# Second MLP of a fused attention kernel: five column passes instead of six, x split in place, operands in one part of SBUF, shorter rings

## The chip, the core and the metric

The kernel runs on one core of a Trainium2 chip. The metric is device time in microseconds (us) of one execution, the median of several runs. TensorE multiplies, VectorE, ScalarE and GpSimd work element by element, SP issues most of the transfers.

## What is computed

Attention over packed queries, then two MLPs on the same 4608 tokens of width 512 (hidden width 2048). The change touches the second MLP alone:

```python
def _moe2_ref(x, w_in, w_out) -> np.ndarray:
    h = x @ w_in
    relu6 = np.clip(h + 3.0, 0.0, 6.0)
    g = h * relu6 / 6.0
    return (g @ w_out).astype(np.float32)

    x = _moe_ref(x=x, **moe_kwargs)
    return _moe2_ref(x=x, **moe2_kwargs)
```

## The kernel before

The first MLP runs in nine blocks of 512 tokens (`block`, with `hidden` at L822 and `project` at L853). It leaves its result x transposed in DRAM, in nine tensors `x1d0` to `x1d8` of 512 columns. Beside it, `Prep` makes the second MLP's weights ready in DRAM.

The second MLP (`class Second`) multiplies with seven products instead of eight on 2 x 2 blocks, in both of its matmuls. A *pass* covers two groups ("halves") of N columns, N = 384, so six passes cover 4608. The two halves are the two block columns; the two halves of the contraction are the two block rows. `x_steps` loads x for a pass (`xr`), forms the differences that the products need, and splits each of the seven operands into a high part (ScalarE, rounded to fp32r) and a low part (VectorE, value minus high part). Both go into one tile, `xc1` to `xc7`. A product of two split operands takes three matmuls: high x high, high x low, low x high.

In a pass, `hidden` (L1031) runs 56 products of 6 matmuls (8 row groups f, 7 products k), applies the activation and leaves `g`. `project` (L1154) is a generator of 28 *steps*, s = 0 to 27, each of 12 matmuls: seven products k in the order 1, 5, 6, 3, 7, 2, 4, and four steps fd for each. So each product is a block of four steps, and at the last of them (s = 3, 7, 11, 15, 19, 23, 27) `after(k)` moves PSUM results out: copies by ScalarE for k = 1, 5 and 2, adds by VectorE for k = 6, 3, 7 and 4, and for k = 7 one add on GpSimd (L1179). An operand of step s is split into a tile `ro` by `split_hi` (ScalarE, L1142) and `split_lo` (VectorE, L1147). Where a product needs a sum of two g blocks, `sums` forms it first.

No scheduler orders this stage: each engine works through its instructions in the order in which the code emits them. In step s of `project` that order is the 12 matmuls, the next weight load, `after(k)` where a block ends, `sums(s + 4)`, the split of step s + 3, one step of `x_steps` for the next pass, and perhaps a `store`:

```python
                self.load_w()
                if s % FD == FD - 1:
                    after(k)
                self.sums(s + 4)
                if s + 3 >= FD:
                    self.split(s + 3)
```

Buffers decide how far ahead this can run: `ro` has four. Weights come through a ring of six tiles `ws` (WS = 6); a tile holds two products of `hidden` or one step of `project`, 12 matmuls either way, and comes in two transfers of 256 KB, one for the first six matmuls and one for the others. After those matmuls `load_w` refills the tile. All these transfers, x and the output stores go through SP's queue in order. x for the next pass is loaded in the middle of `hidden`.

Pools opened with side="right" lie at the upper end of SBUF, the others at the lower end. In the second MLP `ws`, `xr`, `xe` and `xc` are on the right, `ro`, `g` and the rest on the left. In the first MLP `wi`, `wr`, `wo`, `xh`, `xl`, `gh` and `gl` are on the left, `a2h`, `a2l` and `fused` on the right. `hidden` of the first MLP multiplies weight tiles by `a2h` and `a2l`; the weights (products with w_in) lie in `fused` or, for some blocks, in the buffers of `xh` and `xl`.

Of the kernel before, what the change touches and what calls it, by code (L numbers as in the profile page):

```python
# [18 lines left out]
def tile_pack_attention_two_mlps(ctx: ExitStack, tc, q, k, v, p, w_in1, w_out1, w_in2, w_out2, out):  # L19
# [909 lines left out]
    N = 384  # L929
    NPAIR = NBLK * T // (2 * N)  # L930
# [3 lines left out]
    WS = 6  # L934

    class Second:
        def __init__(self):
            right = opened(ctx, "second_r", side="right", reuse_waits="tile")
            self.right = right
            self.prep = None  # L940
            self.extra = []
            self.chunks = self.all_chunks()
            self.loaded, self.used = 0, 0
            self.ws = {}
            self.x = {}
            self.begin = self.x_steps(0)
            self.out = []
# [30 lines left out]
        def x_steps(self, n):  # L978

            xr = self.right.tile([P, KC, 2 * N], F32, tag="xr", name="xr")  # L980
            at_, end = 2 * N * n, 2 * N * (n + 1)
            o = 0
            while at_ < end:
                j, c0 = divmod(at_, T)
                m = min(end - at_, T - c0)
                nc.sync.dma_start(out=xr[:, :, o:o + m], in_=x1d[j][:, :, c0:c0 + m].rearrange("c p t -> p c t"))
                at_, o = at_ + m, o + m
            yield
            b = {(i, k): xr[:, 2 * i:2 * i + 2, k * N:(k + 1) * N] for i in range(2) for k in range(2)}
            e = self.right.tile([P, 2, N], F32, tag="xe", name="xe")  # L990

            def split(k, v):
                t = self.right.tile([P, 2, 2, N], F32R, tag=f"xc{k}", name=f"xc{k}")
                nc.scalar.copy(out=t[:, 0], in_=v)
                nc.vector.tensor_sub(out=t[:, 1], in0=v, in1=f32(t[:, 0]))
                self.x[k] = t


            nc.vector.tensor_sub(out=e, in0=b[1, 1], in1=b[0, 1])
            yield  # L1000
            nc.vector.tensor_sub(out=b[0, 1], in0=b[0, 1], in1=b[0, 0])
            yield
            split(1, b[0, 0])
            yield
            nc.vector.tensor_sub(out=b[0, 0], in0=b[1, 1], in1=b[0, 1])
            yield
            split(6, b[0, 0])
            yield
            split(5, b[0, 1])
            yield  # L1010
            split(7, e)
            yield
            split(3, b[1, 1])
            yield
            nc.vector.tensor_sub(out=b[1, 1], in0=b[1, 0], in1=b[0, 0])
            yield
            split(2, b[1, 0])
            yield
            split(4, b[1, 1])
            yield  # L1020
# [10 lines left out]
        def hidden(self, n):  # L1031
            X, Y, Z, h1, hu, hv = {}, {}, {}, {}, {}, {}
            later = []
# [53 lines left out]
            xs = self.x  # L1087
            for i, (f, k) in enumerate(seq):
# [23 lines left out]
                if i == len(seq) // 2 and self.prep:  # L1112
                    next(self.prep)
# [26 lines left out]
        def split_hi(self, s):  # L1140
            t = self.left.tile([P, 2, 2, N], F32R, tag="ro", name="ro", bufs=4)
            nc.scalar.copy(out=t[:, 0], in_=self.operand(s))  # L1142
            self.ro[s] = t
# [10 lines left out]
        def project(self, n):  # L1154
            X, Y, Z = [], [], []
            o1, ou, ov, o5, oc = (self.left.tile([P, 2, N], F32, tag=tag, name=tag) for tag in ("o1", "ou", "ov", "o5", "oc"))
            last_pair = n == NPAIR - 1
            early = [lambda t=t: self.store(2 * N * n + N + t * P, {0: ou, 1: ov}, t) for t in range(3)]
            if last_pair:
                early += [lambda t=t: self.store(2 * N * n + t * P, {0: oc}, t) for t in range(3)]  # L1160

            def after(k):
                for i in range(2):
                    if k == 1:
                        nc.scalar.copy(out=o1[:, i], in_=X[i])
                    elif k == 5:
                        nc.scalar.copy(out=o5[:, i], in_=Z[i])
                    elif k == 6:
                        nc.vector.tensor_add(out=ou[:, i], in0=o1[:, i], in1=Y[i])
                    elif k == 3:  # L1170
                        nc.vector.tensor_add(out=ou[:, i], in0=ou[:, i], in1=Z[i])
                    elif k == 7:
                        nc.vector.tensor_add(out=ov[:, i], in0=o1[:, i], in1=Y[i])
                    elif k == 2:
                        nc.scalar.copy(out=oc[:, i], in_=X[i])
                    elif k == 4:
                        nc.vector.tensor_add(out=o1[:, i], in0=o1[:, i], in1=Y[i])
                if k == 7:
                    nc.gpsimd.tensor_add(out=ov, in0=ov, in1=o5)  # L1179

            for s in range(FD * S7):
# [26 lines left out]
            for t in range(3):  # L1208
                if last_pair:
                    self.out.append(lambda t=t: self.store(2 * N * n + t * P, {1: o1}, t))  # L1210
                else:
                    self.out.append(lambda t=t: self.store(2 * N * n + t * P, {0: oc, 1: o1}, t))
# [19 lines left out]
        def run(self):  # L1232
            self.left = opened(ctx, "second_l", reuse_waits="tile")
# [279 lines left out]
```

## Time and profile before

| what | us |
|---|---|
| median of 3 runs (1581.17 to 1583.49) | 1583.42 |
| profiled execution, its own time | 1584.56 |
| its span, first to last instruction | 1582.7 |
| TensorE busy / VectorE / ScalarE / GpSimd | 1537.4 / 1037.9 / 810.8 / 194.4 |

The span is what the trace shows; 1.9 us of the execution's time lie around it. The second MLP's first matmul starts at 859.94 us, its last ends at 1576.4. Busy times of TensorE overlap, because a matmul's record runs until its results are out: what counts is the distance between starts. Its clock has two levels, 1.2 and 2.4 GHz, and the profile gives the granted share of the upper.

### The profile page before, as it was taken

Reading aid. Unit: us, or ns where it says so; the run is one execution under the profiler, and the core shown is the slowest. Engines: PE = TensorE matmul, PEld = TensorE weight load, DVE = VectorE, ACT = ScalarE, POOL = GpSimd, SP = SyncE. Lnnn points to the kernel's source line nnn. Section 1 sums busy time; section 2 is a strip of 40 time slices with the busy share of each in tenths; the row PEclk is TensorE's granted clock in tenths of the full one; section 3 lists DMA queues with packets and bytes.
Section 4 is the critical chain, followed back from the end, with each engine's and each line's share of the span. In section 5 each row is a group of like instructions: output and inputs, shape, how many; then the busy total and the mean of one; then the engine's idle time right before and its main releaser. Section 6 shows DMA issues by size and latency. Waiting matters only on the chain.

```text
span 1582.7 us, 23810 instructions
## 1 busy us (share of the span) xinstructions
PE 1537.4 (97%) x8396; PEld 1334.9 (84%) x8396; DVE 1037.9 (66%) x1765; ACT 810.8 (51%) x1360; POOL 194.4 (12%) x172
## 2 busy tenths in 40 slices
PE   6899999999999999999999999999999999999998
PEld 3676766767777777778888999999999999999998
DVE  5876455765577455653443786787787787787775
ACT  4876545654565546654443454454454454454443
POOL 1433011111110111112131000000000000000000
PEclk9899999999999999999999999999999999999999
DMA  8899686887678766757697888988988988988875
GB/s 217 281 273 300 218 232 169 263 215 218 174 227 239 225 162 201 247 172 239 187 335 227 292 255 262 304 254 265 305 252 265 300 256 262 304 252 266 263 256 173
DMA packets 410198, 388.02 MB, mean 245 GB/s; under 512 B 156256, under 2 KB 282976, under 8 KB 410080
## 3 DMA queue, kind: packets, MB, share of 16 engines
q1 hardware_dynamic: 398704, 371.81, 77.6%
q10 hardware_dynamic: 11376, 14.68, 2.8%
q8 instruction: 68, 1.11, 0.3%
q14 instruction: 50, 0.41, 0.1%
HBM read 324.53 MB, written 61.87 MB: 244 GB/s over the span
## 4 chain that ended last, share of the span: by engine, by line
PE 84%; DMA 4%; ACT 3%; DVE 3%; SPq 2%; issue 1%; POOL 1%; POOLq 0%; ACTq 0%; DVEq 0%
PE b L1103 7%; PE b L1105 7%; PE b L1191 7%; PE b L1193 7%; PE b L1104 7%; PE b L1192 7%; PE acc L857 7%; PE acc L858 7%; PE acc L859 7%; PE hps L834 4%; PE hps L836 4%; PE hps L835 4%; PE abank L407 1%; PE abank L495 1%; PE b L1220 1%
## 5 line engine op out<-in xcount | busy, mean ns | idle before, releaser
L1191 PE MATMUL b<-ro,ws 128*128 128x384 f32 x672 | 227.5, 339 | 0.0
L1103 PE MATMUL b<-xc,ws 128*128 128x384 f32 x672 | 226.0, 336 | 0.0
L1193 PE MATMUL b<-ro,ws 128*128 128x384 f32 x672 | 225.9, 336 | 0.0
L1192 PE MATMUL b<-ro,ws 128*128 128x384 f32 x672 | 225.9, 336 | 0.0
L1105 PE MATMUL b<-xc,ws 128*128 128x384 f32 x672 | 224.8, 334 | 0.0
L1104 PE MATMUL b<-xc,ws 128*128 128x384 f32 x672 | 224.7, 334 | 0.0
L850 DVE TENSOR_TENSOR gl<-hps,gh 128x512 fp32r<-128x512 f32 x144 | 98.9, 687 | 166.6 <-ACT gh L849 166.3
L1142 ACT CAST ro<-g 128x768 fp32r<-128x768 f32 x168 | 139.0, 835 | 108.0 <-DVE g L1136 36.5
L1147 DVE TENSOR_TENSOR ro<-g,ro 128x768 fp32r<-128x768 f32 x168 | 159.5, 954 | 12.0 <-ACT ro L1142 11.3
L842 ACT ACTIVATE hps<-hps 128x512 f32<-128x512 f32 x144 | 84.0, 583 | 124.4 <-PE hps L836 121.4
L1192 PEld LDWEIGHTS b<-ro,ws 128*128 128x128 f32 x672 | 126.4, 188 | 0.0
L1191 PEld LDWEIGHTS b<-ro,ws 128*128 128x128 f32 x672 | 126.4, 188 | 0.0
L1193 PEld LDWEIGHTS b<-ro,ws 128*128 128x128 f32 x672 | 126.3, 188 | 0.0
L1104 PEld LDWEIGHTS b<-xc,ws 128*128 128x128 f32 x672 | 126.2, 188 | 0.0
L1103 PEld LDWEIGHTS b<-xc,ws 128*128 128x128 f32 x672 | 126.2, 188 | 0.0
L1105 PEld LDWEIGHTS b<-xc,ws 128*128 128x128 f32 x672 | 126.1, 188 | 0.0
L857 PE MATMUL acc<-gh,wr 128*128 128x512 f32 x288 | 117.5, 408 | 0.0
L857 PE MATMUL acc<-gh,wo 128*128 128x512 f32 x288 | 116.8, 406 | 0.0
L858 PE MATMUL acc<-gl,wr 128*128 128x512 f32 x288 | 113.3, 394 | 0.2 <-DVE gl L850 0.2
L859 PE MATMUL acc<-gh,wr 128*128 128x512 f32 x288 | 113.1, 393 | 0.0
L858 PE MATMUL acc<-gl,wo 128*128 128x512 f32 x288 | 112.7, 391 | 0.0
L859 PE MATMUL acc<-gh,wo 128*128 128x512 f32 x288 | 112.6, 391 | 0.0
(261 smaller groups left out, 3001.4 us busy)
## 6 DMA issues: line engine op xcount, KB each, us to landing
ws<-w2in SPq DMA_DIRECT2D x336, 256.0 KB, 4.2
ws<-w2out SPq DMA_DIRECT2D x336, 256.0 KB, 3.7
wi<-w1i SPq DMA_DIRECT2D x80, 512.0 KB, 5.5
wo<-w1o SPq DMA_DIRECT2D x64, 512.0 KB, 5.7
x1d<-x SPq DMA_DIRECT2D x18, 512.0 KB, 7.3
w1i<-win SPq DMA_DIRECT2D x16, 512.0 KB, 6.8
praw<-in_moe_w_in_dram SPq DMA_DIRECT2D x32, 256.0 KB, 5.8
praw<-in_moe_w_out_dram SPq DMA_DIRECT2D x32, 256.0 KB, 5.2
```

Of the source, the lines that this page charges most:

```text
L850: nc.vector.tensor_sub(out=gl, in0=g, in1=f32(gh))
L857: mm(acc[e], lhsT=w[:, 0, s], rhs=gh, start=first, stop=False)
L858: mm(acc[e], lhsT=w[:, 0, s], rhs=gl, start=False, stop=False)
L859: mm(acc[e], lhsT=w[:, 1, s], rhs=gh, start=False, stop=last)
L1103: mm(ps, lhsT=wh, rhs=xs[k][:, 0, c], start=first, stop=False, skip_group_check=True)
L1104: mm(ps, lhsT=wh, rhs=xs[k][:, 1, c], start=False, stop=False, skip_group_check=True)
L1105: mm(ps, lhsT=wl, rhs=xs[k][:, 0, c], start=False, stop=last, skip_group_check=True)
L1142: nc.scalar.copy(out=t[:, 0], in_=self.operand(s))
L1147: nc.vector.tensor_sub(out=t[:, 1], in0=self.operand(s), in1=f32(t[:, 0]))
L1191: mm(acc[i], lhsT=wh, rhs=ro[:, 0, f], start=first, stop=False, skip_group_check=True)
L1192: mm(acc[i], lhsT=wh, rhs=ro[:, 1, f], start=False, stop=False, skip_group_check=True)
L1193: mm(acc[i], lhsT=wl, rhs=ro[:, 0, f], start=False, stop=last, skip_group_check=True)
```

## The change

- Passes of 512, 512, 512, 384 and 384 columns per half (NS) instead of six of 384. The sum of the columns is the same.
- x: no `xr` and `xe`. Four loads bring the quarters of x straight into the low places of `xc1`, `xc5`, `xc3` and `xc2`; the differences go into the others, and each split is made in place (ScalarE copies the value into the high place, VectorE subtracts that from the value).
- The load of the next x moves from the middle of `hidden` to step 1 of `project`; the four differences to steps 8 to 11, the seven splits to steps 16 to 19 and 24 to 26. Before, the steps between were 1 to 3, 8 to 11 and 16 to 19.
- `ro` moves to a pool on the right (`near`) and has three buffers instead of four (RO = 3), so step s issues the split of step s + 2 and `sums(s + 3)`. The ring of weights has four tiles instead of six (WS = 4).
- The copies for k = 5 go to `ov` instead of an `o5` of its own.
- Stores start at step 21 instead of 22, with N / 128 of them.

```diff
-    N = 384
-    NPAIR = NBLK * T // (2 * N)
+    NS = (512, 512, 512, 384, 384)
+    NPAIR = len(NS)
+    ATS = [2 * sum(NS[:n]) for n in range(NPAIR + 1)]
-    WS = 6
+    WS, RO = 4, 3
...
         def x_steps(self, n):
-            xr = self.right.tile([P, KC, 2 * N], F32, tag="xr", name="xr")
...
+            N = NS[n]
+            def operand(k):
+                t = self.right.tile([P, 2, 2, N], F32R, tag=f"xc{k}", name=f"xc{k}")
+                self.next_x[k] = t
+                return t
+            def load(k, half, side):
+                t = operand(k)
+                at_, o = ATS[n] + side * N, 0
+                while o < N:
+                    j, c0 = divmod(at_ + o, T)
+                    m = min(N - o, T - c0)
+                    nc.sync.dma_start(out=f32(t[:, 1, :, o:o + m]), in_=x1d[j][2 * half:2 * half + 2, :, c0:c0 + m].rearrange("c p t -> p c t"))
+                    o += m
+            def less(k, a, b):
+                if k != a:
+                    operand(k)
+                nc.vector.tensor_sub(out=value(k), in0=f32(value(a)), in1=f32(value(b)))
+            def split(k):
+                t = self.next_x[k]
+                nc.scalar.copy(out=t[:, 0], in_=f32(t[:, 1]))
+                nc.vector.tensor_sub(out=t[:, 1], in0=f32(t[:, 1]), in1=f32(t[:, 0]))
+            for k, half, side in ((1, 0, 0), (5, 0, 1), (3, 1, 1), (2, 1, 0)):
+                load(k, half, side)
             yield
...
+            for k, x, y in ((7, 3, 5), (5, 5, 1), (6, 3, 5), (4, 2, 6)):
+                less(k, x, y)
+                yield
+            for k in (1, 6, 5, 7, 2, 4, 3):
+                split(k)
+                yield
...
-                if i == len(seq) // 2 and self.prep:
-                    next(self.prep)
...
-            t = self.left.tile([P, 2, 2, N], F32R, tag="ro", name="ro", bufs=4)
-            nc.scalar.copy(out=t[:, 0], in_=self.operand(s))
+            v = self.operand(s)
+            t = self.near.tile([P, 2, 2, v.shape[-1]], F32R, tag="ro", name="ro", bufs=RO)
+            nc.scalar.copy(out=t[:, 0], in_=v)
...
                     elif k == 5:
-                        nc.scalar.copy(out=o5[:, i], in_=Z[i])
+                        nc.scalar.copy(out=ov[:, i], in_=Z[i])
...
-                        nc.vector.tensor_add(out=ov[:, i], in0=o1[:, i], in1=Y[i])
+                        nc.vector.tensor_add(out=ov[:, i], in0=ov[:, i], in1=Y[i])
...
-                    nc.gpsimd.tensor_add(out=ov, in0=ov, in1=o5)
+                    nc.gpsimd.tensor_add(out=ov, in0=ov, in1=o1)
...
-                self.sums(s + 4)
-                if s + 3 >= FD:
-                    self.split(s + 3)
-                if self.prep and s and s // FD % 2 == 0:
+                self.sums(s + RO)
+                if s + RO - 1 >= FD:
+                    self.split(s + RO - 1)
+                if self.prep and (s == 1 or s > FD and s // FD % 2 == 0):
                     next(self.prep, None)
-                if s >= FD * 5 + 2 and s - FD * 5 - 2 < len(early):
-                    early[s - FD * 5 - 2]()
+                if s > FD * 5 and early:
+                    early.pop(0)()
...
+            self.near = opened(ctx, "second_n", side="right", reuse_waits="tile")
```

**The order on ScalarE, project, the end of k = 5 (step 7).** `ro` is an operand's split, and the last digit of the g block that it reads is its fd: here 1, 2, 3 of k = 6 are steps 9, 10, 11. Before, in the third pass, and then of the change:

```order
L1142 CAST ro_10386<-g010_9595 128x768
L1142 CAST ro_10405<-g011_9599 128x768
L1167 COPY o5_10240<-b_10349 128x384
L1167 COPY o5_10240<-b_10350 128x384
L1142 CAST ro_10426<-g012_9603 128x768
L1142 CAST ro_10446<-g013_9607 128x768
```

```order
L1141 CAST ro_10411<-g010_9599 128x1024
L1167 COPY ov_10248<-b_10356 128x512
L1167 COPY ov_10248<-b_10357 128x512
L1141 CAST ro_10432<-g011_9603 128x1024
L1141 CAST ro_10453<-g012_9607 128x1024
```

The copies wait for step 7's matmuls. Step 9's high half stood ahead of them and now stands behind them.

**The order on VectorE, project, the end of k = 7 (step 19).** The two L1173 are that block's adds, after which GpSimd's L1179 runs; g100 to g103 are the operands of k = 2, steps 20 to 23. Before, and then of the change:

```order
L1147 TENSOR_TENSOR ro_11899<-g101_10851,ro_11899 128x768
L995 TENSOR_TENSOR xc2_11902<-xr_11204,xc2_11902 128x768
L1173 TENSOR_TENSOR ov_11490<-o1_11488,b_11680 128x384
L1173 TENSOR_TENSOR ov_11490<-o1_11488,b_11681 128x384
L1147 TENSOR_TENSOR ro_11923<-g102_10855,ro_11923 128x768
L995 TENSOR_TENSOR xc4_11926<-xr_11204,xc4_11926 128x768
L1138 TENSOR_TENSOR g010_10846<-g100_10847,g010_10846 128x768
```

```order
L1173 TENSOR_TENSOR ov_10248<-ov_10248,b_10435 128x512
L1173 TENSOR_TENSOR ov_10248<-ov_10248,b_10436 128x512
L1146 TENSOR_TENSOR ro_10675<-g101_9604,ro_10675 128x1024
L1009 TENSOR_TENSOR xc7_10456<-xc7_10456 128x1024
L1146 TENSOR_TENSOR ro_10695<-g102_9608,ro_10695 128x1024
L1136 TENSOR_TENSOR g010_9599<-g100_9600,g010_9599 128x1024
```

Behind the adds the low halves of steps 21 and 22 now follow, with a split of x between them; before it was step 22's, and then the split of x.

**The order on SP, around the load of the next x.** `w2in` and `w2out` are the weights of `hidden` and `project`. Before, in the middle of `hidden`, and then of the change, at step 1 of `project`:

```order
L967 DMA ws_9936<-w2in5_126 128x512
L967 DMA ws_9936<-w2in6_127 128x512
L986 DMA xr_9953<-x1d3_102 128x4x512
L986 DMA xr_9953<-x1d4_103 128x4x256
L967 DMA ws_9963<-w2in5_126 128x512
L967 DMA ws_9963<-w2in6_127 128x512
```

```order
L969 DMA ws_10307<-w2out2_131 128x512
L969 DMA ws_10307<-w2out3_132 128x512
L995 DMA xc1_10310<-x1d4_103 128x2x512
L995 DMA xc5_10312<-x1d5_104 128x2x512
L995 DMA xc3_10314<-x1d5_104 128x2x512
L995 DMA xc2_10316<-x1d4_103 128x2x512
L969 DMA ws_10330<-w2out4_133 128x512
```

Two transfers became four (six for the two passes of 384, whose columns cross from one x1d tensor to the next), now with a tile of `w2out` behind them.

## Rows read from the trace of the kernel before

**Rows 1.** The page, part 1: busy us (share of the span) xinstructions.
```profile
PE 1537.4 (97%) x8396; PEld 1334.9 (84%) x8396; DVE 1037.9 (66%) x1765; ACT 810.8 (51%) x1360; POOL 194.4 (12%) x172
```

**Rows 2.** Stretches, the second MLP: us, busy us (x instructions), granted clock, DMA, GB/s.
```profile
860.00:1574.00 714.00, 714.00 (x4165) 712.80 (x4164) 541.09 (x798) 325.82 (x515) 14.18 (x6) 1.00 0.84 268
```

**Rows 3.** Waits of TensorE, 860 to 1582.7 us: us, times, longest.
```profile
PE b L1220 <- DVE o L1177: 0.2, 1, 0.2
```

**Rows 4.** Timeline, TensorE in hidden, second MLP: start us, us, engine, line, names, shapes.
```profile
1000.58 0.34 PE L1103 MATMUL b<-xc,ws 128*128 128x384 f32 x1
...
1005.78 0.33 PE L1103 MATMUL b<-xc,ws 128*128 128x384 f32 x1
```

**Rows 5.** Timeline, TensorE in the first MLP's last block, both operands left.
```profile
843.61 0.39 PE L834 MATMUL hps<-xh,wi 128*128 128x512 f32 x1
...
849.05 0.39 PE L834 MATMUL hps<-xh,wi 128*128 128x512 f32 x1
```

**Rows 6.** Timeline, TensorE in the first MLP, a2h right, weights left.
```profile
737.60 0.40 PE L834 MATMUL hps<-a2h,xh 128*128 128x512 f32 x1
...
739.00 0.39 PE L857 MATMUL acc<-gh,wo 128*128 128x512 f32 x1
```

**Rows 7.** Timeline, TensorE in the first MLP, both operands right.
```profile
311.71 0.39 PE L835 MATMUL hps<-a2l,fused 128*128 128x512 f32 x1
...
312.62 0.40 PE L836 MATMUL hps<-a2h,fused 128*128 128x512 f32 x1
```

**Rows 8.** Groups by line, second MLP: xcount, busy us, mean ns, idle before.
```profile
L1147 DVE TENSOR_TENSOR ro<-g,ro 128x768 fp32r<-128x768 f32 x168 | 159.5, 954 | 12.0 <-ACT ro L1142 11.3
L1142 ACT CAST ro<-g 128x768 fp32r<-128x768 f32 x168 | 139.0, 835 | 108.0 <-DVE g L1136 36.5 <-DVE g L1138 24.7 <-PE b L1193 20.0
...
L1169 DVE TENSOR_TENSOR ou<-o,b 128x384 f32<-128x384 f32 x12 | 6.4, 554 | 3.0 <-PE b L1193 3.0
...
L1165 ACT COPY o<-b 128x384 f32<-128x384 f32 x12 | 5.7, 479 | 13.6 <-PE b L1193 13.4
```

**Rows 9.** Timeline, project, third pass; step 8's first matmul is at 1173.49.
```profile
1173.23 0.95 ACT L1167 COPY o<-b 128x384 f32<-128x384 f32 x2 [1.23 <-PE b L1193]
...
1173.49 0.34 PE L1191 MATMUL b<-ro,ws 128*128 128x384 f32 x1
...
1174.01 0.34 PE L1191 MATMUL b<-ro,ws 128*128 128x384 f32 x1
...
1174.07 1.57 ACT L1142 CAST ro<-g 128x768 fp32r<-128x768 f32 x2
...
1174.94 0.96 DVE L1147 TENSOR_TENSOR ro<-g,ro 128x768 fp32r<-128x768 f32 x1 [0.41 <-ACT ro L1142]
```

**Rows 10.** Timeline, the same pass; step 16's first matmul is at 1190.13.
```profile
1189.81 1.07 DVE L1171 TENSOR_TENSOR ou<-ou,b 128x384 f32<-128x384 f32 x2 [0.30 <-PE b L1193]
...
1190.13 0.34 PE L1191 MATMUL b<-ro,ws 128*128 128x384 f32 x1
...
1191.67 0.95 DVE L1147 TENSOR_TENSOR ro<-g,ro 128x768 fp32r<-128x768 f32 x1
```

**Rows 11.** Timeline, the same pass; step 20's first matmul is at 1198.45.
```profile
1198.45 0.34 PE L1191 MATMUL b<-ro,ws 128*128 128x384 f32 x1
...
1199.39 2.40 POOL L1179 TENSOR_TENSOR ov<-ov,o 128x768 f32<-128x768 f32 x1 [116.90 <-DVE ov L1173]
...
1200.01 2.61 DVE L995 TENSOR_TENSOR xc<-xr,xc 128x768 fp32r<-128x768 f32 x1
```

**Rows 12.** Tile ws: the two transfers just behind an x load.
```profile
L967 SPq DMA_DIRECT2D ws<-w2in x2: 332/426/520, 1368.6 to 1368.9; - x2
...
DMA to landing us min/median/max: 8.3/8.4/8.6
```

**Rows 13.** Tile ws: all its transfers.
```profile
DMA to landing us min/median/max: 2.7/3.9/9.6
```

**Rows 14.** Stretch 1377 to 1379 us, behind that load; columns as in rows 2.
```profile
1377.00:1379.00 2.00, 2.00 (x14) 2.00 (x13) 1.25 (x3) 0.62 (x1) 0.00 (x0) 1.00 1.05 387
```

More of the change, by code (lines that the diff above doesn't have):

```diff
@@ L920, in load_x @@
             xf[c] = t
-    N = 384
-    NPAIR = NBLK * T // (2 * N)
+    NS = (512, 512, 512, 384, 384)
+    NPAIR = len(NS)
+    ATS = [2 * sum(NS[:n]) for n in range(NPAIR + 1)]
+    assert ATS[-1] == NBLK * T
     ROW = {1: 0, 2: 1, 4: 2, 5: 3, 6: 4, 7: 5, 3: 6}
@@ L944, in __init__ @@
             self.ws = {}
-            self.x = {}
+            self.next_x = {}
             self.begin = self.x_steps(0)
@@ L978, in x_steps @@
         def x_steps(self, n):
-            xr = self.right.tile([P, KC, 2 * N], F32, tag="xr", name="xr")
[L981 to L987, printed above, removed]
-            yield
-            b = {(i, k): xr[:, 2 * i:2 * i + 2, k * N:(k + 1) * N] for i in range(2) for k in range(2)}
@@ L990, in x_steps @@
[L990 to L1019, printed above, removed]
@@ L1020, in x_steps @@
-            yield
+            N = NS[n]
[11 more added lines that the diff above has]
+                    o += m
@@ new lines, in value @@
+            def value(k):
+                return self.next_x[k][:, 1]
+            def less(k, a, b):
[8 more added lines that the diff above has]
+                load(k, half, side)
@@ L1032, in hidden @@
             X, Y, Z, h1, hu, hv = {}, {}, {}, {}, {}, {}
+            N = NS[n]
             later = []
@@ L1086, in hidden @@
             seq = self.order_h()
-            xs = self.x
+            xs, self.next_x = self.next_x, {}
             for i, (f, k) in enumerate(seq):
@@ L1155, in project @@
             X, Y, Z = [], [], []
-            o1, ou, ov, o5, oc = (self.left.tile([P, 2, N], F32, tag=tag, name=tag) for tag in ("o1", "ou", "ov", "o5", "oc"))
+            N = NS[n]
+            o1, ou, ov, oc = (self.left.tile([P, 2, N], F32, tag=tag, name=tag) for tag in ("o1", "ou", "ov", "oc"))
             last_pair = n == NPAIR - 1
-            early = [lambda t=t: self.store(2 * N * n + N + t * P, {0: ou, 1: ov}, t) for t in range(3)]
+            early = [lambda t=t: self.store(ATS[n] + N + t * P, {0: ou, 1: ov}, t) for t in range(N // P)]
             if last_pair:
-                early += [lambda t=t: self.store(2 * N * n + t * P, {0: oc}, t) for t in range(3)]
+                early += [lambda t=t: self.store(ATS[n] + t * P, {0: oc}, t) for t in range(N // P)]
             def after(k):
@@ L1207, in project @@
                     pass
[L1208 to L1212, printed above, removed]
+            for t in range(N // P):
+                self.out.append(lambda t=t: self.store(ATS[n] + t * P, {1: o1} if last_pair else {0: oc, 1: o1}, t))
         def store(self, col, halves, t):
```

## The prediction

> **What bounds the kernel now.** I read the page first: TensorE is busy 97% of the span [rows 1]. Then the stretches: in the second MLP, from 860 to 1574 us, TensorE is busy every microsecond of 714, VectorE 541 and ScalarE 326 of them, and the granted clock is 1.00, the upper of the two levels, 2.4 GHz [rows 2]. Then the waits: TensorE waited there once, 0.2 us, at the very end [rows 3]. So this stage lasts as long as its matmuls are issued, and whatever makes TensorE wait is new time. The last view is the spacing of matmul starts. At 384 columns the 31 starts from 1000.58 to 1005.78 us are 5.20 / 30 = 173.3 ns apart [rows 4]; at 512 columns, in the first MLP, the 25 starts from 843.61 to 849.05 are 5.44 / 24 = 226.7 ns apart [rows 5]. The 128 more columns cost 53.4 ns, 0.417 ns each; so 384 columns take 160 ns, and 13.3 ns come with each matmul, whatever its width.
>
> **Fewer, wider matmuls: -9.0 us.** A pass has 672 matmuls: 56 products of 6 and 28 steps of 12. Before: 6 x 672 x 173.3 = 698.8 us. After: 3 x 672 x 226.7 + 2 x 672 x 173.3 = 689.9 us. The columns are the same; a pass of overheads, 672 x 13.3 ns, goes.
>
> The Trainium skill ("TensorE: Matmul & The Clock Gate", section "Wait — 56ns, not 53.3ns?") gives a fixed cost of about 2.5 ns per warm matmul. By it 672 of them would be worth 1.7 us, and the sum below would end near 1591 us. These matmuls show 13.3 ns at both widths, so the trace disagrees and decides.
>
> **One split less ahead: +6.2 us.** A step of project needs its operand's high half (ScalarE) at its first matmul and the low half (VectorE) at its second. With three buffers the pair for step s + 2 is issued in step s, behind that step's PSUM evacuation; before it was that of s + 3. So after each block's last step there is one step's time for the evacuation and the pair: 12 x 173.3 = 2.08 us at 384, 2.72 at 512, plus one matmul. Durations are 954 and 554 ns on VectorE and 835 and 479 on ScalarE for 768 and 384 elements [rows 8], so by their slopes 1.22 and 1.07 us for 1024.
> - Steps 5 and 9 (after ScalarE's copies). Old: boundary at 1173.49, the copies end at 1174.18, the first low half behind them at 1175.90 [rows 9], 2.41 us after the boundary. That was two steps early enough; now it is wanted after 2.08 + 0.17 = 2.25: 0.16 late. At 512: copy to 0.81, high half to 1.77, low half to 3.02, wanted at 2.95: 0.1 late.
> - Step 17 (after two adds and a sum). Old: the low half ends 1192.62, boundary 1190.13 [rows 10], 2.49 after it: 0.24 late now. At 512: adds to 0.90, sum to 2.04, low half to 3.18: 0.23 late.
> - Step 22. After step 19 GpSimd's add of 2.40 us starts, and VectorE's next operation lasts 2.61 us, not 0.95, ending 0.83 us behind the add [rows 11]. Before, a split of x was caught there, with nothing due soon behind it. Now the split of x stands before the pair of step 22: it ends 4.17 us after the boundary, the low half at 5.04, wanted at 4.33: 0.71 late. At 512 the add takes 3.2 us: from 1.08 to 4.28, x's half to 5.38, the low half to 6.52, wanted at 5.67: 0.85 late.
>
> Steps 13, 21 and 25 have slack by the same count. A wide pass loses 0.1 + 0.1 + 0.23 + 0.85 = 1.3 us, three of them 3.8; the fourth 0.16 x 2 + 0.24 + 0.71 = 1.3; the last, with no next x, 0.6. That is 5.7. With 19 such waits and 0.03 us (ScalarE's end to VectorE's start [rows 9]) to notice each end: 6.2. Bounds: 0, if the work is done in time after all, and 10, if each wait is 0.25 us longer.
>
> **Four weight buffers, and x behind step 1: +3.4 us.** Weights and x share SP's queue. Old: x (1.57 MB) was issued mid-hidden, and the next weight tile, issued one product pair later, landed 8.3 us after its issue (its first half) [rows 12]; the longest of all landings was 9.6, the median 3.9 [rows 13]. Six buffers gave 5 x 2.08 = 10.4 us, so nothing waited. Four give 3 steps: 8.16 us at 512, 6.24 at 384. Once x is through, the queue moves 387 GB/s [rows 14].
> - Passes 1 and 2 load the next pass's 2.10 MB: 0.52 MB more is 1.35 us more, and the tile is issued 0.64 us later (2.72 for 2.08): 8.3 + 1.35 - 0.64 = 9.0 us, against 8.16 + 0.1 already lost: 0.75 late, each.
> - Pass 3 loads 1.57 MB in wide steps: 7.7 us, in time.
> - Pass 4 loads it in steps of 384: 8.3 against 6.24 + 0.16: 1.9 late.
>
> Together 3.4. Below it: 0, if the emptier queue lands x sooner; above it 8.0, with 9.6 for 8.3.
>
> **What I cost at nothing.** The x differences and splits keep their count, 11 per pass, and VectorE and ScalarE have 24% and 54% idle here [rows 2]; their cover is TensorE's issue, and only where they stand before a due split do they count, above. The x load that leaves the middle of hidden frees nothing, since nothing waited for it. 112 weight tiles fewer are landings nobody waited for. The first x, 2.10 MB now, comes in beside the last block of the first MLP; if a split there were late it would cost at most one, 1.2 us. The last pass stays 384 wide, so the tail of stores stays. Moving ro to the right side earns nothing by itself: at 384 columns, with ro on the left and the weights on the right, starts are 0.52 / 3 = 0.173 us apart too, from 1173.49 to 1174.01 [rows 9].
>
> **Sum:** -9.0 + 6.2 + 3.4 = +0.6 us. The profiled execution took 1584.56 us, 1.14 over the median of the runs, 1583.42; so 1585.2 there and **1584.0** as a median. No change: 0.2%, 3.2 us, is about what can be told here.
>
> **Rivals.**
> 1. *The short rings hold.* For it: VectorE and ScalarE are far from full, and the waits of steps 5, 9 and 17 are tenths. If GpSimd's add holds VectorE no longer than the slack (3.3 us gone, and 0.1 of noticing) and only pass 4 waits for weights (1.5 gone): 0.6 - 4.9 = -4.3, 1579.1 us. With no wait at all, 1574.4. Against it: rows 11 show the stop, and the new order puts a due split behind it.
> 2. *The weight ring runs dry.* Mechanism: x's bytes stand before a tile with three steps to come; it decides wherever x's load takes a landing past 8.2 us. At the trace's longest, 9.6 us: 2.05 + 2.05 + 0.7 + 3.2 = 8.0 instead of 3.4: +5.2, 1588.6 us. For it: passes 3 and 4 now cut x into six transfers, with shorter rows. Against it: wide steps ask for weights a quarter slower, so the queue is emptier when x starts.
> 3. *Wide matmuls don't keep 226.7 ns with these operands.* Rows 5 have both operands on the left side. With the moving operand on the right and the weights on the left, seven starts from 737.60 to 739.00 are 1.40 / 6 = 233 ns apart [rows 6]. If the right side behaved so, 2016 x 6.6 ns = 13.3 us more: 1597 us. Against it: with both on the right, 311.71 to 312.62, they are 0.91 / 4 = 227 ns apart [rows 7], and that is where the change puts all of them.
>
> The Trainium skill ("SBUF — State Buffer", section "Who interferes with whom") gives TensorE two independent read ports, one for moving data, one for weights, and has it never wait for anyone; by it rival 3 has no ground. Rows 6 disagree, so it keeps a chance.
>
> **Chances.** The forecast, terms that cancel to within 3.2 us: 0.45. Rival 1: 0.25, all of it faster. Rival 2: 0.22, rival 3: 0.08, both slower. So faster 0.25, same 0.45, slower 0.30. The range goes from 1577, two below rival 1, to 1592, rival 2 with the upper bound of the splits; rival 3 and a kernel without waits, about 0.15, are left out.
>
> **What would show it.** Starts 226.7 ns apart in the wide passes, 173.3 in the others. TensorE's waits in project: on ro's low half at steps 5, 9, 17 and longest at 22, behind GpSimd's add, none there in the last pass; on weight tiles at step 6 of passes 1, 2 and 4. TensorE's idle time in the stage near 9 to 10 us. I am wrong if it is under 5 or over 13, or if the spacing isn't 226.7.

## The result and the profile after

The changed kernel takes 1599.98 us (median of 6 runs, 1596.9 to 1605.34) against 1582.53 for the kernel before: the ratio is 1.0115, interval 1.0096 to 1.0133. It is 17.5 us slower; the forecast was 1584.0, the range ended at 1592. The profiled execution took 1600.19 us with a span of 1598.3, 15.6 us more than the profiled one of before.

The page, part 1, answers to [rows 1]: 672 matmuls are gone, and TensorE is busy for 2.7 us longer.

```profile
PE 1540.1 (96%) x7724; PEld 1249.2 (78%) x7724; DVE 1019.2 (64%) x1630; ACT 797.1 (50%) x1279; POOL 205.9 (13%) x171
```

The stretch of [rows 2] again, with the same columns, and one short stretch in the fourth pass:

```profile
860.00:1574.00 714.00, 700.25 (x3392) 611.36 (x3391) 508.04 (x652) 303.19 (x423) 23.33 (x4) 0.99 0.70 222
...
1422.40:1425.70 3.30, 3.30 (x12) 3.30 (x12) 0.00 (x0) 0.00 (x0) 0.00 (x0) 0.50 0.55 197
```

TensorE was busy all 714 us before; now 13.75 are idle, over the 13 at which the prediction calls itself wrong, and the granted clock is no longer 1.00 throughout: in the short stretch it is 0.50, the lower of the two levels. The waits of TensorE, 855 to 1600 us, answer to [rows 3]; the columns are us, times, longest:

```profile
PE b L1217 <- POOL ov L1179: 8.5, 2, 4.3
PE b L1191 <- DMA ws<-w2out: 4.4, 3, 2.4
PE b L1217 <- DVE o L1177: 0.2, 1, 0.2
```

The largest wait is one that the prediction does not contain: L1217 is the transpose of `store`, and it waits for the add that GpSimd makes behind block 7. In the groups by line and shape that add stands apart by its mean in the wide passes. A low half of `ro` does not (forecast at 1.22 us):

```profile
L1179 POOL TENSOR_TENSOR ov<-ov,o 128x1024 f32<-128x1024 f32 x3 | 20.9, 6979 | 455.1 <-DVE ov L1173 455.1
L1179 POOL TENSOR_TENSOR ov<-ov,o 128x768 f32<-128x768 f32 x2 | 4.5, 2252 | 246.2 <-DVE ov L1173 127.7 <-ACT ro L1141 118.5
...
L1146 DVE TENSOR_TENSOR ro<-g,ro 128x1024 fp32r<-128x1024 f32 x84 | 102.1, 1218 | 45.7 <-ACT ro L1141 45.7
```

**Where the time is.** A step of `project` without a wait is 12 starts at the spacing of its width, 2.72 or 2.08 us. The starts of each step's first matmul (L1191) give what it lost beyond that. In the table the time of the stores' transposes is taken out, as it stands where nothing waits (0.83 us in steps 21 and 22). A step's loss runs to the first matmul of the step behind it: a late weight tile of step 6 counts under step 5, and the stores' transposes count under the step that they stand behind. Steps that aren't named lost nothing.

| lost, us, by pass | 1 | 2 | 3 | 4 | 5 | sum |
|---|---|---|---|---|---|---|
| steps 5 to 7 | 0.98 | 2.01 | 0.25 | 4.55 | 0.34 | 8.1 |
| step 9 | 0.27 | 0.25 | 0.25 | 0.34 | 0.31 | 1.4 |
| step 17 | 0.40 | 0.41 | 0.44 | 0.43 | 0.43 | 2.1 |
| steps 21, 22 | 5.78 | 6.98 | 0.31 | 0.39 | 0 | 13.5 |

That is 25.1 us, where the forecast had 6.2 + 3.4 = 9.6.

The timeline of the first pass at step 21 shows the largest part. First VectorE and GpSimd, then TensorE (start us, us, engine, line, names, shapes, idle before):

```profile
991.66 1.22 DVE L1009 TENSOR_TENSOR xc<-xc 128x1024 fp32r<-128x1024 f32 x1
992.79 1.28 DVE L1173 TENSOR_TENSOR ov<-ov,b 128x512 f32<-128x512 f32 x2
993.99 1.22 DVE L1146 TENSOR_TENSOR ro<-g,ro 128x1024 fp32r<-128x1024 f32 x1
995.12 1.22 DVE L1009 TENSOR_TENSOR xc<-xc 128x1024 fp32r<-128x1024 f32 x1
...
999.66 1.22 DVE L1136 TENSOR_TENSOR g<-g,g 128x1024 f32<-128x1024 f32 x1
...
994.20 8.87 POOL L1179 TENSOR_TENSOR ov<-ov,o 128x1024 f32<-128x1024 f32 x1 [144.18 <-DVE ov L1173]
...
995.77 0.39 PE L1191 MATMUL b<-ro,ws 128*128 128x512 f32 x1
...
998.49 0.38 PE L1217 MATMUL b<-ident,ou 128*128 128x128 f32 x2
1003.13 0.69 PE L1217 MATMUL b<-ident,ov 128*128 128x128 f32 x2 [4.26 <-POOL ov L1179]
1003.47 0.78 PE L1191 MATMUL b<-ro,ws 128*128 128x512 f32 x1
```

VectorE goes from the split of x through the two adds into six more operations without an idle moment (five of them start after 994.20); all but the adds, which read PSUM, have two inputs in SBUF. GpSimd's add is ready at 994.20 and ends at 1003.07, 2.2 us after VectorE ran dry (999.66 + 1.22 = 1000.88). The store behind step 21 needs `ov`, TensorE works in order, and step 22 starts 7.70 us after step 21, 4.98 more than 2.72. The second pass shows the same with 8.84 us.

In the third pass the same add takes 3.23 us. There VectorE was idle for 0.54 us ahead of the two adds, GpSimd came in, and the split of x behind it took 3.16 us in place of 0.95, as in [rows 11]:

```profile
1321.32 1.37 DVE L1173 TENSOR_TENSOR ov<-ov,b 128x512 f32<-128x512 f32 x2 [0.54 <-PE b L1193]
...
1323.74 3.16 DVE L1009 TENSOR_TENSOR xc<-xc 128x768 fp32r<-128x768 f32 x1
...
1322.85 3.23 POOL L1179 TENSOR_TENSOR ov<-ov,o 128x1024 f32<-128x1024 f32 x1 [155.17 <-DVE ov L1173]
```

The second place is the end of step 5 in the fourth pass, where the weights of step 6 are late (its first matmul is the row at 1421.28). SP's queue, then TensorE:

```profile
1410.25 0.80 SPq L969 DMA_DIRECT2D ws<-w2out  x2
1411.14 3.04 SPq L995 DMA_DIRECT2D xc<-x1d  x6
1414.28 1.42 SPq L969 DMA_DIRECT2D ws<-w2out  x2
...
1418.55 0.34 PE L1193 MATMUL b<-ro,ws 128*128 128x384 f32 x1
1421.28 0.41 PE L1191 MATMUL b<-ro,ws 128*128 128x384 f32 x1 [2.40 <-DMA ws<-w2out]
...
1422.41 0.52 PE L1191 MATMUL b<-ro,ws 128*128 128x384 f32 x1
1422.73 0.52 PE L1192 MATMUL b<-ro,ws 128*128 128x384 f32 x1
```

The six transfers of x hold the queue for 3.04 us while they are issued, so the tile of step 6, which stands behind them, goes out at 1414.28, and TensorE waits 2.40 us for it. About 1.1 us after it starts again the spacing goes from 173 to 320 ns for 3.3 us (the stretch at clock 0.50 above): 1.65 us more, in steps 6 and 7.

### The profile page after: what moved, and what is told of

Read it like the earlier page. It is cut to its first block, busy times and chain, and to the rows that moved or that the text cites. A ratio compares the mean times of both kernels' runs of the same rounds, so it can differ in the third digit from the quotient of the medians.

```text
span 1598.3 us, 22012 instructions
## 1 busy us (share of the span) xinstructions
PE 1540.1 (96%) x7724; PEld 1249.2 (78%) x7724; DVE 1019.2 (64%) x1630; ACT 797.1 (50%) x1279; POOL 205.9 (13%) x171
## 4 chain that ended last, share of the span: by engine, by line
PE 80%; DVE 6%; DMA 5%; ACT 3%; SPq 2%; POOL 2%; issue 2%; ACTq 0%; DVEq 0%; POOLq 0%
PE acc L857 7%; PE b L1105 7%; PE b L1103 7%; PE b L1104 7%; PE acc L858 7%; PE acc L859 7%; PE b L1192 6%; PE b L1191 6%; PE b L1193 6%; PE hps L834 4%; PE hps L836 4%; PE hps L835 4%; DMA ws<-w2out 2%; POOL ov L1179 1%; DVE ro L1146 1%
## 5 line engine op out<-in xcount | busy, mean ns | idle before, releaser
L1191 PE MATMUL b<-ro,ws 128*128 128x512 f32 (+1 forms) x560 | 210.3, 376 | 4.4 <-DMA ws<-w2out 4.4
L1192 PE MATMUL b<-ro,ws 128*128 128x512 f32 (+1 forms) x560 | 209.8, 375 | 0.9
L1193 PE MATMUL b<-ro,ws 128*128 128x512 f32 (+1 forms) x560 | 207.8, 371 | 0.0
L1103 PE MATMUL b<-xc,ws 128*128 128x512 f32 (+1 forms) x560 | 207.0, 370 | 0.0
L1105 PE MATMUL b<-xc,ws 128*128 128x512 f32 (+1 forms) x560 | 205.8, 367 | 0.0
L1104 PE MATMUL b<-xc,ws 128*128 128x512 f32 (+1 forms) x560 | 205.6, 367 | 0.0
L1146 DVE TENSOR_TENSOR ro<-g,ro 128x1024 fp32r<-128x1024 f32 (+1 forms) x140 | 156.8, 1124 | 66.1 <-ACT ro L1141 65.8
L1141 ACT CAST ro<-g 128x1024 fp32r<-128x1024 f32 (+1 forms) x140 | 134.0, 964 | 101.4 <-PE b L1193 62.5
L1192 PEld LDWEIGHTS b<-ro,ws 128*128 128x128 f32 x560 | 106.6, 190 | 19.6 <-DVE ro L1146 6.8
L1191 PEld LDWEIGHTS b<-ro,ws 128*128 128x128 f32 x560 | 106.5, 190 | 18.6 <-issue 3.6
L857 PE MATMUL acc<-gh,wr 128*128 128x512 f32 x288 | 118.0, 410 | 0.0
L857 PE MATMUL acc<-gh,wo 128*128 128x512 f32 x288 | 116.9, 406 | 1.0 <-ACT gh L849 1.0
L1193 PEld LDWEIGHTS b<-ro,ws 128*128 128x128 f32 x560 | 106.5, 190 | 13.3
L1179 POOL TENSOR_TENSOR ov<-ov,o 128x1024 f32<-128x1024 f32 (+1 forms) x5 | 25.4, 5088 | 701.3 <-DVE ov L1173 582.8
L1105 PEld LDWEIGHTS b<-xc,ws 128*128 128x128 f32 x560 | 105.1, 188 | 13.2
L1104 PEld LDWEIGHTS b<-xc,ws 128*128 128x128 f32 x560 | 105.2, 188 | 13.0
L1103 PEld LDWEIGHTS b<-xc,ws 128*128 128x128 f32 x560 | 105.1, 188 | 12.9
```

The source lines that it names most:

```text
L857: mm(acc[e], lhsT=w[:, 0, s], rhs=gh, start=first, stop=False)
L1103: mm(ps, lhsT=wh, rhs=xs[k][:, 0, c], start=first, stop=False, skip_group_check=True)
L1104: mm(ps, lhsT=wh, rhs=xs[k][:, 1, c], start=False, stop=False, skip_group_check=True)
L1105: mm(ps, lhsT=wl, rhs=xs[k][:, 0, c], start=False, stop=last, skip_group_check=True)
L1146: nc.vector.tensor_sub(out=t[:, 1], in0=self.operand(s), in1=f32(t[:, 0]))
L1191: mm(acc[i], lhsT=wh, rhs=ro[:, 0, f], start=first, stop=False, skip_group_check=True)
```

## Experiments

Theory A, from the trace: VectorE in the wide passes comes into block 7's adds with a queue behind it, keeps GpSimd out until it runs dry, and the early store makes TensorE wait. Beside it stand the two terms of the forecast, short lookahead and late weights. Runs 1 to 7 change one part of the changed kernel each, runs 8 and 10 two, and run 9 changes the kernel before; ratios are to the kernel before, timed beside it.

**1. The add on VectorE.**

```diff
-                    nc.gpsimd.tensor_add(out=ov, in0=ov, in1=o1)
+                    nc.vector.tensor_add(out=ov, in0=ov, in1=o1)
```

> The last of the three adds behind block 7 (ov += o1) goes from GpSimd to VectorE, nothing else. Theory A: in the first two passes GpSimd's add takes 8.8 us because VectorE, with five operations one behind the other, lets it in only when it runs dry; the early store at step 21 waits for it, and TensorE behind the store (4.6 us in step 21, then 1.1 and 2.4 us of matmuls at the lower clock in step 22). On VectorE the add takes about 1.2 us and ends before step 21 does, so steps 21 and 22 of these passes lose what the other wide pass loses: 12 us go, about 1588 us. Rival B: the store itself, or x's splits ahead of it, make step 21 late whoever adds: no gain, or up to 1.2 us per pass lost to the longer VectorE queue, 1600 to 1606. Waits for weights (steps 5 to 7) stay under both.

Measured: 1588.44 us, ratio 1.0035 (1.0024 to 1.0045), 11.5 us less than the changed kernel. TensorE's waits, 850 to 1600 us:

```profile
PE b L1191 <- DMA ws<-w2out: 3.3, 3, 2.0
PE b L1192 <- DVE ro L1146: 1.4, 5, 0.4
...
```

The store waits no more. Instead step 21 of every pass is 0.5 to 0.7 us late on its low half, since the add now stands ahead of that split in VectorE's queue. The wait went with the add, as theory A has it, and rival B falls.

**2. The early stores one step later.**

```diff
-                if s > FD * 5 and early:
+                if s > FD * 5 + 1 and early:
```

> The early stores start behind step 22, as in the kernel before, instead of behind step 21; GpSimd keeps its add. Theory A (VectorE keeps GpSimd out while it has work): the add ends no sooner than 15.5 us after step 18's start, step 22 now ends at 13.6, so at least 1.9 us of wait remain in each of the first two passes and about 2.7 go, with part of the slow clock: 1590 to 1595 us. If VectorE, no longer held up by TensorE, stays packed longer, the add ends later still and less is gained. Rival C (the add takes 8.8 us only because the store or its transposes meet it): the add is back at 3.2 us, no wait, 1588 us.

Measured: 1597.51 us, ratio 1.0095 (1.0078 to 1.0112): its interval overlaps the changed kernel's, so little or nothing was gained, less than the 5 to 10 us expected. VectorE's last operation of the row and GpSimd's add, first pass:

```profile
1002.48 1.22 DVE L1136 TENSOR_TENSOR g<-g,g 128x1024 f32<-128x1024 f32 x1
...
994.75 11.14 POOL L1179 TENSOR_TENSOR ov<-ov,o 128x1024 f32<-128x1024 f32 x1 [144.66 <-DVE ov L1173]
```

TensorE no longer stops at step 21, so VectorE gets the work of step 22 as well, stays packed until 1003.70, and the add ends 2.19 us behind that, at 1005.89. The wait only moved to step 22 (4.50 us longer than 12 matmuls). So the step at which the store stands isn't the cause, and rival C falls.

**3. Six weight buffers.**

```diff
-    WS, RO = 4, 3
+    WS, RO = 6, 3
```

> The ring of weights is 6 deep, as in the kernel before, instead of 4 (the last buffer of the split ring then lies below the top 96 KB). If x's load ahead of the weight tiles was what made steps 5 to 7 of passes 1, 2 and 4 late, the waits for weights there go: 0.6 + 1.6 + 2.6 us and 1.9 us of slower matmuls behind them, 6.7 in all, about 1593 us. Rival: the queue itself is late whatever the ring's depth: less than 2 us gained. If the buffer below the top 96 KB costs by its place, every third step of the wide passes shows starts more than 226.7 ns apart.

Measured: 1591.07 us, ratio 1.0047 (1.0032 to 1.0062). TensorE's waits:

```profile
PE b L1217 <- POOL ov L1179: 8.5, 2, 4.3
...
PE b L1192 <- DVE ro L1146: 0.2, 1, 0.2
```

No wait for weights is left, and the 8.5 us for `ov` stay. Steps 5 now lose 0.25 to 0.31 us, the splits' share; so the weights' share in the table is 8.1 - 1.4 = 6.7 us, 1.9 of it matmuls at a lower pace behind a wait. The "top 96 KB" of the expectation are what the change fills on the right side, per partition: seven `xc` and three `ro` of 8 KB, four `ws` of 4 KB. With six `ws` the last `ro` lies below these 96 KB, and no step is longer for it.

**4. Four split buffers.**

```diff
-    WS, RO = 4, 3
+    WS, RO = 4, 4
```

> The ring of split operands is 4 deep, as in the kernel before, instead of 3, so each pair is issued one step earlier. The waits on split halves at steps 5, 9, 17 and (third and fourth pass) 22 go: 1.4 + 1.4 + 2.1 + 0.7 = 5.6 us. Theory A (VectorE has work queued, GpSimd starves): the deeper ring gives VectorE more work that is ready, so the add of the first two passes is still 5 us or more and step 21 still waits: about 1594 us. Rival D (GpSimd starves only because the short ring lets VectorE fall behind): the add is 3.2 us again and steps 21 and 22 lose nothing more: about 1582 us. Waits for weights stay under both.

Measured: 1579.62 us, ratio 0.998 (0.9969 to 0.9991). Theory A's number was 1594; rival D's, 1582, is 2.4 us off. First pass:

```profile
991.78 1.37 DVE L1173 TENSOR_TENSOR ov<-ov,b 128x512 f32<-128x512 f32 x2 [0.27 <-PE b L1193]
993.07 1.22 DVE L1146 TENSOR_TENSOR ro<-g,ro 128x1024 fp32r<-128x1024 f32 x1
994.21 3.42 DVE L1009 TENSOR_TENSOR xc<-xc 128x1024 fp32r<-128x1024 f32 x1
...
993.28 3.26 POOL L1179 TENSOR_TENSOR ov<-ov,o 128x1024 f32<-128x1024 f32 x1 [143.99 <-DVE ov L1173]
```

One step more of lookahead lets VectorE finish the split of x and then wait 0.27 us for TensorE ahead of the adds. GpSimd comes in, and steps 5 (but for weights), 9, 17, 21 and 22 lose nothing. So the starved add is itself a consequence of the short split ring: it puts VectorE a step behind. What theory A expected here, that a deeper ring gives VectorE more ready work and keeps GpSimd out, falls. TensorE still waits 3.1 us for weights, in passes 2 and 4.

**5. Both rings back.**

```diff
-    WS, RO = 4, 3
+    WS, RO = 6, 4
```

> The changed kernel with both rings at their old depth, 6 weight buffers and 4 split buffers; they no longer all lie in the top 96 KB (two split buffers lie below it). With four split buffers alone 1579.6 us were left, 3.55 of it late weights and slower matmuls behind them in passes 2 and 4. If the two short rings are all that the change lost, these go too: no wait of TensorE in the stage, 1576 us, which is also the old time less the 9 us of the 672 matmul overheads that went (1574). Rival: operands below the top 96 KB cost by their place once nothing else makes the steps late: every step with such a buffer is longer than 12 x 226.7 ns, up to 12 x 6.6 ns each in half of the wide steps, 3 us in all, 1579 to 1580.

Measured: 1575.53 us against 1584.76 for the kernel before in the same comparison, ratio 0.9942 (0.9927 to 0.9957): faster than both kernels. By the medians it is 24.5 us less than the changed kernel (26.7 with each taken against the kernel before beside it); the table above counts 25.1. TensorE's waits in the stage are the one of before:

```profile
PE b L1217 <- DVE o L1177: 0.2, 1, 0.2
```

No step of any pass is longer than its 12 matmuls and its stores, though two of the four `ro` buffers now lie below the top 96 KB. So the place of these operands costs nothing that shows.

**6. No split of x at step 19.**

```diff
-                if self.prep and (s == 1 or s > FD and s // FD % 2 == 0):
+                if self.prep and s != FD * 5 - 1 and (s == 1 or s > FD and s // FD % 2 == 0):
```

> Both rings stay short; only the split of x that stands at step 19 is left out there, so it and the ones behind it come one step later each (the last at step 27). Theory E: GpSimd's add is kept out in passes 1 and 2 because VectorE came into block 7's adds with a queue behind it, without an idle moment since step 19; in all passes in which VectorE was idle for 0.3 us or more ahead of these adds GpSimd came in behind the operation that was running. With one operation of 1.2 us less ahead of them VectorE waits for TensorE there, the add takes about 3.2 us, steps 21 and 22 lose no more than in the third pass: 12 us go, about 1588. Rival: it is VectorE's load after the adds (steps 20 and 21, the same number of operations as before) that keeps GpSimd out: the add stays at 8 us or more, 1598 to 1601.

Measured: 1594.45 us, ratio 1.006 (1.0044 to 1.0076). First pass:

```profile
991.92 1.28 DVE L1173 TENSOR_TENSOR ov<-ov,b 128x512 f32<-128x512 f32 x2
...
997.66 1.22 DVE L1136 TENSOR_TENSOR g<-g,g 128x1024 f32<-128x1024 f32 x1
...
993.33 7.74 POOL L1179 TENSOR_TENSOR ov<-ov,o 128x1024 f32<-128x1024 f32 x1 [143.98 <-DVE ov L1173]
```

Both numbers of the expectation were missed, since the edit did not do what it was meant to: a split issued at step 19 stands behind the adds in VectorE's queue, so the adds are still entered without an idle moment. With one operation less behind them VectorE runs dry at 998.88, and the add again ends 2.19 us later, at 1001.07. The load behind the adds sets how long GpSimd waits. Whether it waits at all had to be tried with the split of step 18, which stands ahead of them.

**7. No split of x at step 18.** The same edit with `s != FD * 5 - 2`.

> Again one split of x is moved out of block 7 (the last then stands at step 27), this time the one issued at step 18, which VectorE did just ahead of block 7's adds (in the run without the split of step 19 it still went into the adds without an idle moment, and GpSimd's add ended 2.2 us after VectorE ran dry). Theory E, mended: whether GpSimd gets in is set by an idle moment of VectorE ahead of the adds; how long it waits otherwise by the work behind them. Here VectorE ends its split at 4.1 us after step 18's start and waits for TensorE until 5.0; behind the adds it has the same work as the changed kernel. So GpSimd's add takes 3.2 us in the wide passes too, and steps 21 and 22 lose at most what the third pass loses: 12 us go, 1588. Rival: the load behind the adds alone decides: 8.8 us as in the changed kernel, 1600.

Measured: 1587.84 us, ratio 1.0026 (1.0016 to 1.0036), as expected. First pass:

```profile
991.96 1.37 DVE L1173 TENSOR_TENSOR ov<-ov,b 128x512 f32<-128x512 f32 x2 [0.83 <-PE b L1193]
...
993.46 3.26 POOL L1179 TENSOR_TENSOR ov<-ov,o 128x1024 f32<-128x1024 f32 x1 [144.60 <-DVE ov L1173]
```

Behind the adds stand the same operations as in the changed kernel; ahead of them VectorE waits 0.83 us for TensorE. The add takes 3.26 us, and no store waits.

**8. The loads of x spread over four steps, four split buffers.**

```diff
-    WS, RO = 4, 3
+    WS, RO = 4, 4
...
                 load(k, half, side)
-            yield
+                if n or k == 2:
+                    yield
...
-                if self.prep and (s == 1 or s > FD and s // FD % 2 == 0):
+                if self.prep and (1 <= s <= FD or s > FD and s // FD % 2 == 0):
```

> Four weight buffers as in the change, four split buffers; the four loads of x are issued behind steps 1, 2, 3 and 4, one each, instead of all behind step 1. Theory: weights come late at steps 5 to 7 because 1.6 to 2.1 MB of x stand in the queue ahead of one weight tile, not because four buffers are too few; with 0.5 MB ahead of each tile, 0.8 MB per step of 2.7 us, the queue (387 GB/s) keeps up and the waits (3.55 us in the run with four split buffers alone) go: 1576 us, and no wait longer than 0.3 us on a weight tile. Rival: four buffers are too few as soon as anything stands in the queue: waits at steps 4 to 8, 1579 or more. The differences of x, from step 9 on, must not be late.

Measured: 1576.84 us, ratio 0.9953 (0.9937 to 0.997). The longest landing of a weight tile is 7.4 us (9.7 in the changed kernel), 6.1 within the second MLP, and TensorE's waits are again

```profile
PE b L1218 <- DVE o L1178: 0.2, 1, 0.2
```

Here four weight buffers were enough with no more than 0.5 MB of x ahead of a tile; only steps 8 and 9 of the fourth pass lose 0.4 us together.

**9. The kernel before with three split buffers.**

```diff
-            t = self.left.tile([P, 2, 2, N], F32R, tag="ro", name="ro", bufs=4)
+            t = self.left.tile([P, 2, 2, N], F32R, tag="ro", name="ro", bufs=3)
...
-                self.sums(s + 4)
-                if s + 3 >= FD:
-                    self.split(s + 3)
+                self.sums(s + 3)
+                if s + 2 >= FD:
+                    self.split(s + 2)
```

> The kernel before with three split buffers instead of four and the pairs issued one step later, nothing else: 384 columns, 6 weight buffers, x loaded in the middle of hidden, stores from step 22. It prices the one-step-less term alone. By what the passes of 384 columns in the changed kernel lost: 0.31 at step 5, 0.31 at step 9, 0.41 at step 17 in each of six passes and 0.4 at step 22 in five, 8.2 us: 1591. By the prediction's own arithmetic 0.16 + 0.16 + 0.24 (six times) and 0.71 (five times): 6.9, 1590. If GpSimd's add is kept out here too (VectorE without an idle moment ahead of block 7's adds), it takes 5 us or more and the store at step 22 waits: 2 us and more per pass on top, 1600 or later.

Measured: 1594.28 us, ratio 1.0059 (1.0044 to 1.0074), 9.5 us, 3 us more than either number of the expectation and 6 less than the rival's. Each pass loses 0.32 us at step 5, 0.31 at 9, 0.40 at 17, and all but the last 0.88 at step 22, which was expected at 0.4 or 0.71: 10.6 us in the profile. TensorE's waits name only the last kind:

```profile
PE b L1192 <- DVE ro L1147: 3.0, 5, 0.6
```

GpSimd's add keeps its 2.4 us, although VectorE comes into the adds without an idle moment here too (second pass; behind the adds it ran straight on):

```profile
1078.34 0.95 DVE L995 TENSOR_TENSOR xc<-xr,xc 128x768 fp32r<-128x768 f32 x1
1079.21 1.01 DVE L1173 TENSOR_TENSOR ov<-o,b 128x384 f32<-128x384 f32 x2
...
1080.39 2.41 POOL L1179 TENSOR_TENSOR ov<-ov,o 128x768 f32<-128x768 f32 x1 [118.79 <-DVE ov L1173]
```

So at 384 columns GpSimd comes in either way, as in the fourth pass of the changed kernel; the idle moment of run 7 made the difference in the wide passes, and is not a rule for every width. The short split ring alone makes the old kernel slower too, at the four steps that the prediction names.

**10. The add on VectorE, the loads of x spread, both rings short.** Edits 1 and 8, with `WS, RO = 4, 3`.

> The rings as short as in the change, all operands in the top 96 KB; the add of block 7 on VectorE, and the four loads of x behind steps 1, 2, 3 and 4. Both repairs gained what they should alone (the add on VectorE 12 us of 1600; the spread loads left no wait for weights). If they are independent, the waits on weights (3.5 us with the add on VectorE) go too and what is left is the shorter lookahead: about 0.3 at steps 5 and 9, 0.4 at 17 and 0.5 to 0.9 at 21 or 22 per pass, 7.5 us, 1584 to 1585, no faster than the kernel before. Rival: four weight buffers with a step's weights less ahead and splits late at the same steps (5) still leave a wait for weights, 1587 or more.

Measured: 1584.22 us, ratio 1.0008 (0.9998 to 1.0017), as expected. The two repairs add up, but by the step starts of the profile the short lookahead still costs 7.9 us, which eats most of the 9.0 that the forecast gives the fewer matmuls:

```profile
PE b L1193 <- DVE ro L1147: 1.5, 5, 0.4
...
```

## Why the prediction was wrong

**Fewer, wider matmuls, -9.0 us: right.** In run 5, where nothing waits, the stretch from the stage's first matmul to its last lasts 705.99 us (861.03 to 1567.02), against 714.72 before (859.94 to 1574.67): -8.7. The Trainium skill ("TensorE: Matmul & The Clock Gate", section "Wait — 56ns, not 53.3ns?") has 2.5 ns per matmul, by which the prediction estimates 1.7 us. The trace disagrees: 8.7 us for 672 matmuls are 13.0 ns each.

**One split less ahead, +6.2 us: the waits were right, its step 22 was not.** Steps 5, 9 and 17 wait as forecast, and step 22 in passes 3 and 4; together they lost 1.4 + 1.4 + 2.1 + 0.7 = 5.6 us. Each is longer than forecast by 0.1 to 0.2 us (0.25 for 0.1 at step 5), and step 22 shorter (0.31 for 0.85). The first pass at step 5 shows why a wait of a few hundredths costs a quarter:

```profile
950.36 0.39 PE L1193 MATMUL b<-ro,ws 128*128 128x512 f32 x1
950.59 0.39 PE L1191 MATMUL b<-ro,ws 128*128 128x512 f32 x1
950.92 0.50 PE L1192 MATMUL b<-ro,ws 128*128 128x512 f32 x1
951.25 0.39 PE L1193 MATMUL b<-ro,ws 128*128 128x512 f32 x1
```

VectorE's low half ends at 950.86, some 0.04 us after its matmul was due at 950.82. That matmul starts 0.10 us late (0.33 behind its neighbour, not 0.227), and the next one loses another 0.10. I had put 0.03 on that.

**The step that failed** is the sentence "At 512 the add takes 3.2 us: from 1.08 to 4.28". I priced how GpSimd's add stops VectorE, from [rows 11], and never that VectorE's row can stop the add. In passes 1 and 2 it took 8.9 and 8.8 us. Nor does the prediction price that the early store, which needs this add, moves from step 22 to step 21; run 2 shows that its old place would not have helped. The sum therefore lacks 12.8 us: 5.78 + 6.98. Of these 1.2 and 2.4 are step 22's matmuls at a lower granted clock behind the wait (0.72 from 1003.5 to 1007.8 us, 0.54 from 1168.1 to 1173.6). This term alone carries the result out of the range.

**Weights, +3.4 us: right in place, too small.** Waits came ahead of step 6 in passes 1, 2 and 4 and not in 3, as forecast, and they cost 6.7 us (forecast 0.75, 0.75, 0 and 1.9; measured 0.7, 1.8, 0 and 4.2). In pass 2 the tile took 9.5 us to land, where the forecast had 9.0. In pass 4 it landed sooner than the 8.3 us of the forecast, 6.9 after its issue, and was later all the same. Two things were left out there: issuing the six transfers of pass 4 takes 3.04 us of SP's queue, so the next tile is not issued at step 2's end (1412.3, two steps of 2.08 us and 0.2 behind step 1's first matmul at 1407.98) but at 1414.28; and 1.65 us of slower matmuls follow that wait.

**The tail, costed at nothing, got 1.7 us shorter.** The early stores of the last pass start a step earlier. From the last product's matmul to the end of the span it was 8.0 us before (1574.67 to 1582.7) and is 6.3 now (1592.04 to 1598.3).

```profile
1574.67 0.34 PE L1193 MATMUL b<-ro,ws 128*128 128x384 f32 x1
...
1578.41 0.38 ACT L1222 ACTIVATE st<-b 128x256 f32<-128x256 f32 x1 [1.69 <-DMA out_dram<-st]
```

These two rows are of the kernel before: its last evacuation waited 1.69 us for an output buffer that an early store still held. In the changed kernel the last product's matmul starts at 1592.04, and no evacuation behind it waits for a buffer.

**A misreading without effect.** The prediction's "112 weight tiles fewer" are 56 tiles of two transfers each.

**The sum, with what was measured:** -8.7 + 5.6 + 6.7 + 12.8 - 1.7 = +14.7 us. The stage starts 0.9 us later in this profile (860.80 for 859.94), which makes the 15.6. That start lies between 856.7 and 862.0 us in the other profiles, so the 0.9 is not put down to the change.

**The rivals.** Rival 1 (the rings hold) fell: every wait came. Rival 2 (the weight ring runs dry) is true in its mechanism: it had 8.0 us for the weights, and 6.7 came, about a quarter of the 25.1 lost. Rival 3 (wide matmuls slower with these operands) fell: starts lie 0.227 us apart wherever nothing waits, and run 5 shows no step that is longer by its operands' place. [Rows 6] did not carry it either: the last matmul there (L857) has both operands on the left, and it and the five behind it, which have them there too, start 0.23 us apart as well (739.00 to 740.16).

## What to carry to other kernels

When a ring gets shorter, redo the order of every engine that fills it as a whole: one step less of lookahead does not only make the consumer late, it also takes away the idle moments of the engines that fill the ring, and an engine that got its turn in them may lose it. Where an operation on GpSimd feeds an in-order engine, price also the case that it ends only behind VectorE's unbroken row, and not its mean in the old trace alone. And here the wide passes were worth their saved matmul overheads only with the split ring at its old depth: with both rings restored they gained 9.2 us (1575.53 for 1584.76), with four weight buffers and x's loads spread 7.9 (1576.84), and with both rings short, repairs and all, nothing (run 10).

## What was not expected of the hardware

In the third pass of the changed kernel a split of x took 3.16 us instead of 0.95 and ended 0.82 us behind GpSimd's add: the two did not run side by side. The Trainium skill ("SBUF — State Buffer", section "Who interferes with whom") has VectorE operations with two inputs in SBUF contend with a GpSimd instruction that reads SBUF, and whoever issues first gets the shared ports for the whole instruction. The third pass agrees. The first two passes do not: there the add, recorded from 994.20, should by that rule have come in ahead of the split that starts at 995.12. What surprised is that VectorE kept GpSimd out for a whole row: through four operations and more, each recorded as starting some 0.08 us before the one ahead of it ends, GpSimd did not come in between any two; its add ended 2.2 us after the row in runs 2 and 6 and in the changed kernel, at 11.14, 7.74 and 8.87 us. In the wide passes this split cleanly: where VectorE had not been idle ahead of the two adds (the first two passes of the changed kernel and of runs 2, 3 and 6) the add was shut out, and where it had been idle for 0.27 us or more it came in behind one operation. In the narrow passes it came in even without an idle moment (run 9). What in the hardware decides it the traces don't show, and it stays open.

A wait does not always cost the clock. In run 6 step 21 is 3.70 us longer than its 2.72 in both of the first two passes. Just behind that, in step 22, the granted clock was 0.64 in the one and 1.00 in the other:

```profile
1001.30:1006.10 4.80, 4.80 (x19) 3.79 (x18) 2.36 (x2) 1.53 (x2) 0.00 (x0) 0.64 0.16 58
1164.10:1167.30 3.20, 3.20 (x19) 2.67 (x18) 1.34 (x2) 1.53 (x2) 0.00 (x0) 1.00 0.22 82
```

The same 19 matmul records take 4.8 us or 3.2. The changed kernel's runs spread over 8.4 us, those of run 5, in which nothing waits, over 1.4 (1574.92 to 1576.29). The mean granted clock of the first lies between 0.984 and 0.989, that of the second is 0.991 in every run; that the clock behind the waits makes the difference in spread is likely, but was not tried.
